# Weight loads placed around the token gathers, and the PSUM banks of the routing stage dealt out anew

## The chip, the cores and the metric

The kernel runs on one core of a Trainium2 chip. The time is device microseconds (us) of one execution, the median of several runs. Engines are named as the profile names them: PE (TensorE, matrix products), DVE (VectorE), ACT (ScalarE), POOL (GpSimd) and SP (SyncE, which issues most DMAs). A bank is one of the eight PSUM banks of 128 x 512 f32.

## The reference

Three layers follow each other: a recurrent attention with gates over 2 x 768 tokens (8 heads of 40), then a mixture of 8 experts in which each expert takes exactly 192 of the 1536 tokens, then a dense mixture of 4 experts.

```python
logits = x @ w_gate                        # x: 1536 x 320, 8 experts
order = np.argsort(-logits.flatten())
for idx in order:                          # best (token, expert) pair first
    tok, e = int(idx) // E, int(idx) % E
    if assigned[tok] >= 0 or counts[e] >= cap:   # cap = 192
        continue
    assigned[tok] = e
    counts[e] += 1
for e in range(E):
    mask = assigned == e
    out[mask] = np.maximum(x[mask] @ w1[e], 0) @ w2[e]      # 320 -> 1024 -> 320
...
p = domain_probs / (domain_probs.sum(-1, keepdims=True) + 1e-09)
for e in range(4):                         # second mixture: all tokens, all experts
    out += p[:, e:e+1] * (np.maximum(x @ w1[e], 0) @ w2[e])
```

## The kernel before, in words

**Three stages.** `attention` writes its rows, padded to 388 columns, to `x_dram` in HBM (L430). `routing` (L617) assigns the tokens, gathers each expert's 192 rows back from `x_dram` and runs the first mixture; its results `X2h` and `X2l` stay in SBUF as two parts of reduced precision. The second mixture (L1262 on) multiplies all tokens by all four experts in three products each.

**The assignment.** There are eight phases, `ph` 0 to 7; a phase fills one expert. `search` (L678) looks for the key value at which one expert reaches 192 tokens, digit by digit, in seven rounds `d`. A round is: twelve small matmuls count tokens above 31 candidates into `pc` (L688); DVE marks which candidates reach 192 in `hit` and `flag` (L709); one matmul with a matrix of ones sums the marks into `pj` (L712), which is the digit; DVE compares the keys with the next candidates around that digit (L719, `cmp`) and then, behind it, moves the base `bt` on to the next digit (L724). In round 5 it forms `kk` (L728) in place of `bt`. `pc` and `pj` are tiles of two banks, `pr` and `pn`. After round 6 the winner is masked out and `offsets` (L810) numbers its tokens. Phase 7 takes what is left (`final`, L819).

**What follows a phase.** `follow` (L1050) runs `dispatch` (L866): it turns the slots into token numbers `tok`, and POOL issues two indirect DMAs (L910, the gathers `xg`, 128 rows of 1552 bytes each). `prep` (L917) transposes the rows on PE (L930) into `xt`. Then `moe1` (L939), a job, has for each of eight blocks `f` of 128 hidden units a product over the last 64 inputs (`thirds`, L953, in two groups of four blocks), two over the first 256 (`main`, L959), a ReLU on ACT (L962), and the second layer (`second`, L972, three blocks behind, and `second3`, L980). The hidden sums `Z` share three banks z0 to z2, and the second group of `thirds` stands behind `main(3)`. The second layer's sums `y0`, `y1` reuse the banks that the job before has left only when DVE has read them for `X2l` (L1003, L1010).

**Weights.** `fetch` (L838), at the end of a search, has SP read the expert's number and issue the load of its first layer's weights (L845, 1280 KB). `fetch2` (L851) issues the second layer's (L857, 1280 KB): right behind for every phase but 0, and in phase 0 between the two gathers, with the number copied by DVE (L854). `split2` (L578) loads the second mixture's weights in pieces `raw` (L592) into six buffers, and splits them on ACT, DVE and POOL. Its first `next` issues the six loads of expert 0; it stands in front of the search of phase 6 (`CR['SP']`, L1185). The loads for expert 1 stand behind everything in `routing` in SP's queue and wait for free buffers only.

**The order.** Each engine runs its instructions in program order. `run` (L1095) and `drain` (L1136) write that order: they keep a reckoned clock of each engine, and put jobs, dispatches and transposes into gaps of the search by assumed costs and due times: `CR['GA']` 3000 ns from a gather's issue to its rows, 1040 ns of POOL for a gather (L915), 5000 ns for the second weights. In phases 0 and 1, while no job exists, PE gaps are filled with dummy matmuls (L1130).

Of the kernel before, what the change touches and what calls it, by code (L numbers as in the profile page):

```python
# [7 lines left out]
F32 = mybir.dt.float32  # L8
F32R = mybir.dt.float32r
BF = mybir.dt.bfloat16  # L10
# [21 lines left out]
BIG = 1e35  # L32
CR = {'D': 0, 'W6': 9, 'SO': 2, 'SC': 3, 'W': 14, 'W0': 5, 'W1': 5, 'W2': 5000, 'W3': (2, 2), 'W4': 4, 'W5': 2, 'X': 4, 'Y': 1, 'L': (6000, 14000), 'GA': 3000, 'WA': 8000, 'VP': 100, 'PV': 190, 'A': (330, 330, 500), 'B': (800, 600, 400), 'SX': 4, 'SP': 6, 'AB': 330}

# [12 lines left out]
def tile_mlstm_moe_moe(ctx: ExitStack, tc: tile.TileContext, gates, gatex, qk, kv, og, wgate, dprob,  # L47
# [26 lines left out]
    cands = [ct([P, NC if d < 6 else 4], BF, name=f"cand{d}") for d in range(1, 7)]  # L74
    onesd = [ct([P, P], BF, name=f"ones{d}") for d in range(6)]
    mask = ct([P, 6], I32, name="mask")
    fold = ct([P, P], name="fold")
    iota16 = ct([P, 16], name="iota16")
# [11 lines left out]
    def routing_consts(pool):  # L90
# [21 lines left out]
        G.memset(crow[0:1, 1:2], float(CAP))  # L112
        G.memset(gone, 0.0)
        for t in cmps + flag + [oa, tk]:
            G.memset(t, 0.0)
        for d, t in enumerate(onesd):
            G.memset(t, 32.0 ** -d)
            G.memset(mask[:, d:d + 1], 31 << (22 - 5 * d) if d < 5 else 3)
        G.memset(erem, float(E1 * (E1 + 1) // 2))
# [27 lines left out]
    last = keys.tile([P, E1], BF, name="last")  # L147
    cmps = [keys.tile([P, NT * NC + P - NC], BF, name=f"cmp{i}") for i in range(2)]
    gone = keys.tile([P, NT], F32, name="gone")
# [467 lines left out]
    def routing():  # L617
        with ExitStack() as st:
# [16 lines left out]

            def pn():
                return ps_r.tile([P, 512], F32, name="pn")

            def side_of(k):
                cmps.reverse()  # L640
                return cmps[0], cmps[0][:, :NT * k].rearrange("p (c k) -> p c k", k=k)

# [7 lines left out]
            def pick(ph):  # L650
# [6 lines left out]
                dgs = pool.tile([P, 6, NT], F32, name="dgs")  # L657
                b1 = pool.tile([P, NT], F32, name="b1")
                kb = top.bitcast(I32)
                out = {"dgs": dgs, "b1": b1}  # L660

                def first():
# [8 lines left out]
                                                      mask[:, :, None].to_broadcast([P, 6, NT]), OP.bitwise_and),  # L671
                              lambda: V.tensor_scalar(dgs, dg, 2.0 ** -27, None, op0=OP.mult),
                              lambda: V.scalar_tensor_tensor(b1, d0, 16.0, dgs[:, 0], op0=OP.add, op1=OP.add)]
                if ph:
# [3 lines left out]
            def search(ph):  # L678
                k = PICK.pop()
                dgs, bt, cmp = k["dgs"], k["b1"], k["cmp"]  # L680
                oh = ohs[ph % 2]
                ready = k.get("ready", clock["V"] + VP)
                for d in range(7):
                    pc = pr()
                    m = NC if d < 6 else 4
                    yield "P", ready - 60, 400 if d < 6 else 280
                    for c in range(NT):
                        T.matmul(pc[:, :E1], cmp[:, m * c:m * c + P], oh[:, c], start=(c == 0), stop=(c == NT - 1))  # L688
                    end = clock["P"] - 80
                    if d == 1:  # L690
                        eo = rt.tile([P, NT, E1], F32, name="eo")
                        V.tensor_mul(eo, oh, bc(erow))
                        on("V", 169)
# [10 lines left out]
                    yield "V", end + PV  # L704
                    pj = pn()
                    if d < 6:
                        fl = flag[d % 2]
                        hit = rt.tile([P, E1], BF, name="hit")
                        V.tensor_scalar(hit[:NC], pc[:NC, :E1], float(CAP), 0.0, op0=OP.is_ge, op1=OP.max,  # L709
                                        accum_out=fl[:NC])  # L710
                        yield "P", on("V", 165) + VP + 30, 110
                        T.matmul(pj[:, 0:1], onesd[d], fl, start=True, stop=True)  # L712
                        yield "V", clock["P"] + PV - 80
                        n = pj[:, 0:1]
                        cand = cands[d]
                        k = cand.shape[1]
                        cmp, v = side_of(k)
                        w = [P, NT, k]
                        V.scalar_tensor_tensor(v, cand[:, None, :].to_broadcast(w), n,  # L719
                                               bt[:, :, None].to_broadcast(w), op0=OP.add, op1=OP.is_le)  # L720
                        ready = on("V", 490 if d < 5 else 190) + 150
                        if d < 5:
                            b2 = rt.tile([P, NT], F32, name="bt")
                            V.scalar_tensor_tensor(b2, bt, n, dgs[:, d + 1], op0=OP.subtract, op1=OP.add)  # L724
                            bt = b2
                        else:
                            kk = rt.tile([P, NT], F32, name="kk")
                            V.tensor_scalar(kk, bt, n, 2.0 ** 31, op0=OP.subtract, op1=OP.mult)  # L728
                        on("V", 150)
# [80 lines left out]
            def offsets(tot, both=True):  # L810
                po = pn()
# [23 lines left out]

            WI, R0 = {}, {}

            def fetch(ph):  # L838
# [7 lines left out]
                XW[ph] = clock["V"] + CR['WA']  # L846
                R0[ph] = r0
                if ph:
                    fetch2(ph)

            def fetch2(ph):  # L851
                if not ph:
                    wi = rt.tile([P, 1], I32, name="wi2", bufs=1)
                    V.tensor_scalar(wi[:1], WI[ph][:1], 0, None, op0=OP.add)  # L854
                    R0[ph] = nc.values_load(wi[0:1, 0:1], engines=[mybir.EngineType.SP], min_val=0,
                                            max_val=(E1 - 1) * P)
                nc.sync.dma_start(W2[ph], m1w2[bass.ds(R0[ph], P), :])  # L857
                XW2[ph] = max(clock["V"] + 1000, XW[ph]) + CR['W2']

# [6 lines left out]
            def dispatch(ph):  # L866
# [41 lines left out]
                for k, (ti, r0, n, s0) in enumerate(pt):  # L908
# [30 lines left out]
            def moe1(ph):  # L939
# [35 lines left out]
                def second3():  # L975
                    for f in range(NF):
                        if f % 4 == 0:
                            yield 1040, H[NF - 1][1]
# [4 lines left out]
                yield from thirds(0)  # L983
# [376 lines left out]
```

## Time and profile before

| | us |
|---|---|
| runs of the kernel | 636.54, 636.74, 651.99 (median 636.74) |
| the profiled execution | 640.5 |
| its span, first to last instruction | 638.4 |
| PE busy | 606.0 (95%) |
| weight loads of PE | 512.7 (80%) |
| DVE busy | 263.4 (41%) |
| ACT busy | 180.5 (28%) |
| POOL busy | 62.9 (10%) |
| chain that ended last: PE 71%, issue 11%, DMA 7%, DVE 6% | |

The busy share of PE is a mean over stages: a slice with the digit 9 in the page's timeline has PE at work nine tenths of the time or more, but at whichever of its two clock levels was granted. The chain of waits is followed back from the last instruction; "DMA xg<-x_dram,tok" has 4% of the span in it.

### The profile page before, as it was taken

What the parts mean: (1) busy time and instruction counts of PE and PEld (TensorE: products, weight loads), DVE (VectorE), ACT (ScalarE), POOL (GpSimd) and SP (SyncE); (2) the same over time, 40 slices, a digit from 0 to 9 for tenths busy, and PEclk for the clock granted to TensorE, in tenths of its full rate; (3) what the DMA queues carried; (4) which work ended last, traced back from release to release, by engine and by line L of the source; (5) the groups of instructions that cost most, each with busy time, mean ns of one, the idle gap of its engine ahead of it and who ended that gap; (6) DMA issues with size and microseconds to landing.
All of it is one profiled execution on the core that took longest, in us unless ns stands there. A gap on an engine that the chain in (4) does not pass through costs nothing.

```text
span 638.4 us, 11154 instructions
## 1 busy us (share of the span) xinstructions
PE 606.0 (95%) x4475; PEld 512.7 (80%) x4478; DVE 263.4 (41%) x952; ACT 180.5 (28%) x472; POOL 62.9 (10%) x120
## 2 busy tenths in 40 slices
PE   7999899799999796999999999999999999999996
PEld 4889764588778685988888888888888888888886
DVE  7767687456666344012322132413224231312231
ACT  7899210122222133323221123311133211111120
POOL 4000001011101113001200001100011000002022
PEclk9999899699999898899999999999999999999999
DMA  7855412435443647201220002300000000001011
GB/s 198 246 138 139 116 38 92 149 142 190 183 174 120 278 177 303 82 1 34 66 84 1 1 0 68 97 17 1 1 1 2 1 1 0 1 1 41 1 42 41
DMA packets 13883, 52.18 MB, mean 82 GB/s; under 512 B 3592, under 2 KB 5544, under 8 KB 11240
## 3 DMA queue, kind: packets, MB, share of 16 engines
q1 hardware_dynamic: 11864, 46.16, 21.6%
q0 software_dynamic: 1600, 5.15, 2.5%
q8 instruction: 35, 0.57, 0.4%
q10 hardware_dynamic: 368, 0.17, 0.1%
q14 instruction: 16, 0.13, 0.1%
HBM read 46.99 MB, written 4.35 MB: 80 GB/s over the span
## 4 chain that ended last, share of the span: by engine, by line
PE 71%; issue 11%; DMA 7%; DVE 6%; ACT 2%; POOL 1%; POOLq 0%; SPq 0%; DVEq 0%; ACTq 0%
PE y L1236 9%; PE y L1238 8%; PE y L1237 8%; PE z L1220 7%; PE z L1222 7%; PE z L1221 6%; PE y L972 4%; DMA xg<-x_dram,tok 4%; PE z L959 4%; PE z L1224 3%; PE px L372 3%; PE z L1229 2%; PE st L336 2%; PE pr L688 2%; DMA raw<-in_m2w_dram 1%
## 5 line engine op out<-in xcount | busy, mean ns | idle before, releaser
L1278 DVE SCALAR_TENSOR_TENSOR h2l<-z,h2h 128x512 fp32r<-128x512 f32 x96 | 66.4, 692 | 238.6 <-ACT h2h L1277 238.6
L1277 ACT ACTIVATE h2h<-z 128x512 fp32r<-128x512 f32 x96 | 57.5, 599 | 262.7 <-PE z L1224 192.2
L1236 PE MATMUL y<-wh,h2h 128*128 128x320 f32 x384 | 120.9, 315 | 0.0
L1238 PE MATMUL y<-wh,h2l 128*128 128x320 f32 x384 | 118.5, 309 | 0.0
L1237 PE MATMUL y<-wl,h2h 128*128 128x320 f32 x384 | 118.5, 309 | 0.0
L1236 PEld LDWEIGHTS y<-wh,h2h 128*128 128x128 f32 x384 | 72.0, 188 | 11.2 <-issue 7.9
L1220 PE MATMUL z<-X2h,wh 128*128 128x512 f32 x192 | 76.9, 401 | 0.8 <-DVE X2l L1010 0.8
L1222 PE MATMUL z<-X2h,wl 128*128 128x512 f32 x192 | 75.9, 395 | 0.0
L1221 PE MATMUL z<-X2l,wh 128*128 128x512 f32 x192 | 75.7, 394 | 0.0
L1237 PEld LDWEIGHTS y<-wl,h2h 128*128 128x128 f32 x384 | 72.1, 188 | 3.2
L1238 PEld LDWEIGHTS y<-wh,h2l 128*128 128x128 f32 x384 | 72.1, 188 | 0.0
L959 PE MATMUL z<-xt,w 128*128 128x192 f32 x256 | 59.7, 358 | 0.0
L972 PE MATMUL y<-h,w 128*128 128x192 f32 x256 | 56.9, 344 | 2.0 <-DVE X2l L1003 2.0
L959 PEld LDWEIGHTS z<-xt,w 128*128 128x128 f32 x256 | 45.3, 205 | 1.8 <-issue 0.7
L972 PEld LDWEIGHTS y<-h,w 128*128 128x128 f32 x256 | 41.8, 193 | 4.0 <-DVE X2l L1003 2.6
L1222 PEld LDWEIGHTS z<-X2h,wl 128*128 128x128 f32 x192 | 36.2, 189 | 9.3
L962 ACT ACTIVATE h<-z 128x192 f32<-128x192 f32 x64 | 21.2, 331 | 79.1 <-PE z L959 74.2
L611 POOL TENSOR_TENSOR wl<-raw,wh 128x512 fp32r<-128x512 f32 x16 | 20.6, 1286 | 232.5 <-ACT wh L601 215.5
L1220 PEld LDWEIGHTS z<-X2h,wh 128*128 128x128 f32 x192 | 36.0, 188 | 6.3 <-DVE X2l L1010 1.1
L1221 PEld LDWEIGHTS z<-X2l,wh 128*128 128x128 f32 x192 | 36.1, 188 | 4.5
L1224 PE MATMUL z<-X2h,wh 128*128 128x512 f32 x96 | 38.0, 396 | 0.0
L688 PEld LDWEIGHTS <-cmp 128*128 128x128 bf16 x588 | 20.4, 98 | 11.6 <-DVE cmp L719 6.1
(260 smaller groups left out, 774.5 us busy)
## 6 DMA issues: line engine op xcount, KB each, us to landing
w<-in_m1w_dram SPq DMA_DIRECT2D x16, 1280.0 KB, 6.4
raw<-in_m2w_dram SPq DMA_DIRECT2D x20, 512.0 KB, 9.4
qk<-in_qk_dram SPq DMA_DIRECT2D x4, 832.0 KB
kv<-in_kv_dram SPq DMA_DIRECT2D x5, 648.0 KB, 5.2
x_dram<-xr SPq DMA_DIRECT2D x12, 194.0 KB, 2.3
qk<-in_qk_dram SPq DMA_DIRECT2D x4, 416.0 KB
sig<-in_og_dram SPq DMA_DIRECT2D x1, 1280.0 KB
raw<-in_m2w_dram SPq DMA_DIRECT2D x4, 256.0 KB, 8.6
```

The costliest lines, as they stand in the source:

```text
L688: T.matmul(pc[:, :E1], cmp[:, m * c:m * c + P], oh[:, c], start=(c == 0), stop=(c == NT - 1))
L959: T.matmul(Z[f], w1[:, k * F + f * P:k * F + (f + 1) * P], xt[:, k], start=False, stop=(k == 1), skip_group_check=True)
L972: T.matmul(Y[0][:, i * CAP:(i + 1) * CAP], w2[:, f * DM + i * P:f * DM + (i + 1) * P], h, start=(f == 0 and i == 0), stop=(f == NF - 1), s ...
L1220: T.matmul(z, hi[:, c], xh[:, k], start=(opens and k == 0), stop=False, skip_group_check=True)
L1221: T.matmul(z, hi[:, c], xl[:, k], start=False, stop=False, skip_group_check=True)
L1222: T.matmul(z, lo[:, c], xh[:, k], start=False, stop=False, skip_group_check=True)
L1224: T.matmul(z, hi[:, c], xh[:, 2], start=False, stop=not opens, skip_group_check=True)
L1236: T.matmul(y[:, :DM], hh[:, ts], hi[:, c], start=(f == 0), stop=False)
L1237: T.matmul(y[:, :DM], hh[:, ts], lo[:, d], start=False, stop=False)
L1238: T.matmul(y[:, :DM], hl[:, ts], hi[:, c], start=False, stop=(f == NF - 1))
L1277: A.activation(hh, z, AF.Relu)
L1278: V.scalar_tensor_tensor(hl, z, 0.0, hh.bitcast(F32), op0=OP.max, op1=OP.subtract)
```

## The change

- The first `next(spl)`, with the six loads of the second mixture's expert 0, stands in front of the search of phase 0.
- `fetch` issues only the first layer's weights. `fetch2` is called in every phase behind both gathers of `dispatch`; the expert's number is copied on POOL, so that SP waits for POOL there.
- The marks of round `d` are kept in rows 32*(d%4) on of one of two `flag` columns, cleared by DVE in rounds 0 and 4; the counts of the round land in those rows, since the window of `cmp` is moved left by `g` columns. One matmul sums all marks so far with two matrices of ones in place of six. The keys' first three digits are kept as prefixes, so that `bt` is a view in rounds 0 to 2. Round 3 forms `bt` ahead of its comparison and round 5 forms `kk` ahead of it; rounds 3 and 4 add the next digit behind it.
- `pj` is columns 16 to 31 of the round's `pc`, and `pn` is gone; the first expert layer has four banks, z0 to z3. All eight blocks of `thirds` stand at the start of a job.
- The planner's assumed costs of a gather (1250 ns of POOL, 2800 ns to the rows) and of the grouped products change.

```diff
         for t in cmps + flag + [oa, tk]:
             G.memset(t, 0.0)
-        for d, t in enumerate(onesd):
-            G.memset(t, 32.0 ** -d)
-            G.memset(mask[:, d:d + 1], 31 << (22 - 5 * d) if d < 5 else 3)
+        G.memset(onesd[1], 0.0)
+        for d in range(6):
+            G.memset(onesd[d // 4][32 * (d % 4):32 * (d % 4) + 32], 32.0 ** -d)
+            G.memset(mask[:, d:d + 1], -(1 << (22 - 5 * d)) if d < 3 else 31 << (22 - 5 * d) if d < 5 else 3)
...
-                              lambda: V.tensor_scalar(dgs, dg, 2.0 ** -27, None, op0=OP.mult),
-                              lambda: V.scalar_tensor_tensor(b1, d0, 16.0, dgs[:, 0], op0=OP.add, op1=OP.add)]
+                              lambda: V.scalar_tensor_tensor(dgs, dg, 2.0 ** -27, off[:, :, None].to_broadcast([P, 6, NT]),
+                                                             op0=OP.mult, op1=OP.add)]
...
-                        T.matmul(pc[:, :E1], cmp[:, m * c:m * c + P], oh[:, c], start=(c == 0), stop=(c == NT - 1))
+                        T.matmul(pc[:, :E1], cmp[:, 96 + m * c - g:96 + m * c - g + P], oh[:, c], start=(c == 0), stop=(c == NT - 1))
                     end = clock["P"] - 80
+                    if d in (0, 4):
+                        V.memset(flag[d // 4], 0.0)
+                        on("V", 60)
...
-                    pj = pn()
+                    pj = pc[:, 16:32]
                     if d < 6:
-                        fl = flag[d % 2]
+                        fl = flag[d // 4]
+                        r = slice(g, g + NC)
...
-                        T.matmul(pj[:, 0:1], onesd[d], fl, start=True, stop=True)
+                        T.matmul(pj[:, 0:1], onesd[d // 4], fl, start=True, stop=True)
...
+                        if d < 3:
+                            bt = dgs[:, d]
+                        if d == 3:
+                            bt = rt.tile([P, NT], F32, name="bt")
+                            V.scalar_tensor_tensor(bt, dgs[:, 2], n, dgs[:, 3], op0=OP.subtract, op1=OP.add)
+                            on("V", 210)
+                        elif d == 5:
+                            kk = rt.tile([P, NT], F32, name="kk")
+                            V.tensor_scalar(kk, bt, n, 2.0 ** 31, op0=OP.subtract, op1=OP.mult)
+                            on("V", 100)
...
-                        if d < 5:
+                        if d in (3, 4):
                             b2 = rt.tile([P, NT], F32, name="bt")
-                            V.scalar_tensor_tensor(b2, bt, n, dgs[:, d + 1], op0=OP.subtract, op1=OP.add)
+                            V.tensor_add(b2, bt, dgs[:, d + 1])
                             bt = b2
...
-                R0[ph] = r0
-                if ph:
-                    fetch2(ph)
+                XW2[ph] = XW[ph] + CR['W2']
 
             def fetch2(ph):
-                if not ph:
-                    wi = rt.tile([P, 1], I32, name="wi2", bufs=1)
-                    V.tensor_scalar(wi[:1], WI[ph][:1], 0, None, op0=OP.add)
-                    R0[ph] = nc.values_load(wi[0:1, 0:1], engines=[mybir.EngineType.SP], min_val=0,
-                                            max_val=(E1 - 1) * P)
-                nc.sync.dma_start(W2[ph], m1w2[bass.ds(R0[ph], P), :])
-                XW2[ph] = max(clock["V"] + 1000, XW[ph]) + CR['W2']
+                wi = rt.tile([P, 1], I32, name="wi2")
+                G.tensor_scalar(wi[:1], WI[ph][:1], 0, None, op0=OP.add)
+                r0 = nc.values_load(wi[0:1, 0:1], engines=[mybir.EngineType.SP], min_val=0, max_val=(E1 - 1) * P)
+                nc.sync.dma_start(W2[ph], m1w2[bass.ds(r0, P), :])
+                XW2[ph] = max(on("G", 100) + 1000, XW[ph]) + CR['W2']
...
-                    if not ph and not k:
-                        fetch2(ph)
-                    XR[ph, ti] = on("G", 1040, clock["V"] + 200) + CR['GA']
+                    XR[ph, ti] = on("G", 1250, clock["V"] + 200) + CR['GA']
+                fetch2(ph)
...
-                def thirds(f0):
-                    yield 1040, r0
-                    for i in range(2):
-                        z = ps_m.tile([P, 512], F32, name=f"z{(f0 // 2 + i) % 3}")
-                        for j in range(2):
-                            Z[f0 + i + 2 * j] = z[:, j * CAP:j * CAP + CAP]
-                    for f in range(f0, f0 + 4):
+                def thirds():
+                    zs = [ps_m.tile([P, 512], F32, name=f"z{i}") for i in range(4)]
+                    for f in range(NF):
+                        if f % 4 == 0:
+                            yield 1040 - f * 48, r0
                         r = f % 2 * 64
                         c = 2 * F + f // 2 * P
-                        T.matmul(Z[f], w1[r:r + 64, c:c + P], xt[r:r + 64, 2], start=(f < f0 + 2), stop=False,
+                        Z[f] = zs[f % 4][:, f // 4 * CAP:f // 4 * CAP + CAP]
+                        T.matmul(Z[f], w1[r:r + 64, c:c + P], xt[r:r + 64, 2], start=(f < 4), stop=False,
                                  skip_group_check=True)
...
-                    if f == 3:
-                        yield from thirds(4)
...
+            next(spl)
             for ph in range(E1):
-                if ph == CR['SP']:
-                    next(spl)
                 run(search(ph) if ph < E1 - 1 else final(ph), ph)
```

## Rows read from the trace of the kernel before

**Rows 1.** Busy time by stretch, second mixture: us, engines' busy us, PEclk, DMA share.

```profile
286.20:605.80 319.60, 319.59 (x1767) 276.27 (x1768) 92.08 (x155) 70.43 (x122) 24.16 (x27) 1.00 0.07 21
```

**Rows 2.** Waits of PE, 91 to 287 us: us in total, times, longest.

```profile
PE t L930 <- DMA xg<-x_dram,tok: 13.5, 7, 4.6
PE y L972 <- DVE X2l L1003: 2.0, 2, 1.4
```

**Rows 3.** Timeline of PE: start, us; in brackets idle before and releaser.

```profile
117.53 0.48 PE L930 MATMUL t<-ident,xg 128*128 128x128 f32 x1 [3.33 <-DMA xg<-x_dram,tok]
...
218.15 0.69 PE L930 MATMUL t<-ident,xg 128*128 128x128 f32 x2 [4.63 <-DMA xg<-x_dram,tok]
...
254.45 0.66 PE L930 MATMUL t<-ident,xg 128*128 128x128 f32 x2 [4.27 <-DMA xg<-x_dram,tok]
```

**Rows 4.** Timeline of POOL: gathers of phases 0, 3, 5 and 7.

```profile
109.51 1.35 POOL L910 DMA_INDIRECT xg<-x_dram,tok  x1 [17.60 <-DVE wi L854]
111.17 0.95 POOL L910 DMA_INDIRECT xg<-x_dram,tok  x1 [0.31 <-DVE hit L709]
...
173.53 0.95 POOL L910 DMA_INDIRECT xg<-x_dram,tok  x1 [0.30 <-issue]
...
209.81 0.94 POOL L910 DMA_INDIRECT xg<-x_dram,tok  x1 [14.49 <-PE z L959]
...
247.38 0.96 POOL L910 DMA_INDIRECT xg<-x_dram,tok  x1 [2.55 <-DVE tok L907]
```

**Rows 5.** Timeline of SP's queue: weight loads around those gathers.

```profile
110.15 0.35 SPq L857 DMA_DIRECT2D w<-in_m1w_dram  x1
...
203.37 3.03 SPq L592 DMA_DIRECT2D raw<-in_m2w_dram  x6
...
243.23 0.33 SPq L857 DMA_DIRECT2D w<-in_m1w_dram  x1
243.68 53.18 SPq L592 DMA_DIRECT2D raw<-in_m2w_dram  x7
```

**Rows 6.** Tile xg, stretches around the gathers of phases 0, 3, 5, 7.

```profile
DMA to landing us min/median/max: 6.8/7.4/8.0
...
DMA to landing us min/median/max: 3.0/3.1/3.1
...
DMA to landing us min/median/max: 8.0/8.2/8.3
...
DMA to landing us min/median/max: 6.8/6.9/6.9
```

**Rows 7.** Line L857, all eight loads of the second weights.

```profile
DMA to landing us min/median/max: 7.0/7.5/8.0
```

**Rows 8.** Busy time in short stretches, last three columns PEclk, DMA share, GB/s.

```profile
111.00:111.25 0.25, 0.25 (x3) 0.13 (x2) 0.02 (x1) 0.00 (x0) 0.08 (x1) 0.50 2.10 328
176.00:176.25 0.25, 0.25 (x3) 0.25 (x2) 0.25 (x1) 0.00 (x0) 0.00 (x0) 1.00 0.14 50
```

**Rows 9.** Timeline of DVE: the number copied for SP in phase 0.

```profile
109.20 0.13 DVE L854 TENSOR_SCALAR wi<-wi 1x1 int32<-1x1 int32 x1
```

**Rows 10.** Busy time in short stretches: where PEclk falls or rises.

```profile
108.50:109.00 0.50, 0.50 (x9) 0.27 (x6) 0.32 (x3) 0.00 (x0) 0.00 (x0) 0.66 0.10 41
...
125.50:126.00 0.50, 0.50 (x4) 0.50 (x3) 0.22 (x1) 0.33 (x1) 0.00 (x0) 0.78 0.41 82
...
224.00:225.00 1.00, 1.00 (x16) 0.84 (x14) 0.17 (x2) 0.33 (x1) 0.00 (x0) 0.65 0.00 0
...
258.00:259.00 1.00, 1.00 (x6) 1.00 (x5) 0.00 (x0) 0.84 (x4) 0.55 (x1) 0.58 0.00 0
```

**Rows 11.** Timeline of PE: job 0's second layer begins; a group of `thirds`.

```profile
126.29 0.90 PE L972 MATMUL y<-h,w 128*128 128x192 f32 x4
...
274.66 0.92 PE L953 MATMUL z<-xt,w 64*128 64x192 f32 x8
```

**Rows 12.** Timeline of DVE in the search of phase 0: `bt` and `kk`.

```profile
98.09 0.23 DVE L724 SCALAR_TENSOR_TENSOR bt<-bt,pn,dgs 128x12 f32<-128x12 f32 x1
...
100.92 0.23 DVE L728 TENSOR_SCALAR kk<-bt,pn 128x12 f32<-128x12 f32 x1
```

More of the change, by code (lines that the diff above doesn't have):

```diff
@@ L32 @@
 BIG = 1e35
-CR = {'D': 0, 'W6': 9, 'SO': 2, 'SC': 3, 'W': 14, 'W0': 5, 'W1': 5, 'W2': 5000, 'W3': (2, 2), 'W4': 4, 'W5': 2, 'X': 4, 'Y': 1, 'L': (6000, 14000), 'GA': 3000, 'WA': 8000, 'VP': 100, 'PV': 190, 'A': (330, 330, 500), 'B': (800, 600, 400), 'SX': 4, 'SP': 6, 'AB': 330}
+CR = {'D': 0, 'W6': 9, 'SO': 2, 'SC': 3, 'W': 14, 'W0': 5, 'W1': 5, 'W2': 5000, 'W3': (2, 2), 'W4': 4, 'W5': 2, 'X': 4, 'Y': 1, 'L': (6000, 14000), 'GA': 2800, 'WA': 8000, 'VP': 100, 'PV': 190, 'A': (330, 330, 500), 'B': (800, 600, 400), 'SX': 4, 'AB': 330}
 def weave(gens):
@@ L74, in tile_mlstm_moe_moe @@
     cands = [ct([P, NC if d < 6 else 4], BF, name=f"cand{d}") for d in range(1, 7)]
-    onesd = [ct([P, P], BF, name=f"ones{d}") for d in range(6)]
+    onesd = [ct([P, P], BF, name=f"ones{d}") for d in range(2)]
     mask = ct([P, 6], I32, name="mask")
+    off = ct([P, 6], name="off")
     fold = ct([P, P], name="fold")
@@ L113, in routing_consts @@
         G.memset(gone, 0.0)
+        G.memset(off, 0.0)
+        G.memset(off[:, :3], 16.0)
         for t in cmps + flag + [oa, tk]:
             G.memset(t, 0.0)
-        for d, t in enumerate(onesd):
-            G.memset(t, 32.0 ** -d)
-            G.memset(mask[:, d:d + 1], 31 << (22 - 5 * d) if d < 5 else 3)
+        G.memset(onesd[1], 0.0)
+        for d in range(6):
+            G.memset(onesd[d // 4][32 * (d % 4):32 * (d % 4) + 32], 32.0 ** -d)
+            G.memset(mask[:, d:d + 1], -(1 << (22 - 5 * d)) if d < 3 else 31 << (22 - 5 * d) if d < 5 else 3)
         G.memset(erem, float(E1 * (E1 + 1) // 2))
@@ L147, in tile_mlstm_moe_moe @@
     last = keys.tile([P, E1], BF, name="last")
-    cmps = [keys.tile([P, NT * NC + P - NC], BF, name=f"cmp{i}") for i in range(2)]
+    cmps = [keys.tile([P, 96 + NT * NC + P - NC], BF, name=f"cmp{i}") for i in range(2)]
     gone = keys.tile([P, NT], F32, name="gone")
@@ L634, in pr @@
                 return ps_r.tile([P, 512], F32, name="pr")
-            def pn():
-                return ps_r.tile([P, 512], F32, name="pn")
             def side_of(k):
                 cmps.reverse()
-                return cmps[0], cmps[0][:, :NT * k].rearrange("p (c k) -> p c k", k=k)
+                return cmps[0], cmps[0][:, 96:96 + NT * k].rearrange("p (c k) -> p c k", k=k)
             def compare(u, cand):
@@ L657, in pick @@
                 dgs = pool.tile([P, 6, NT], F32, name="dgs")
-                b1 = pool.tile([P, NT], F32, name="b1")
                 kb = top.bitcast(I32)
-                out = {"dgs": dgs, "b1": b1}
+                out = {"dgs": dgs}
                 def first():
@@ L679, in search @@
                 k = PICK.pop()
-                dgs, bt, cmp = k["dgs"], k["b1"], k["cmp"]
+                dgs, cmp = k["dgs"], k["cmp"]
                 oh = ohs[ph % 2]
@@ L685, in search @@
                     m = NC if d < 6 else 4
+                    g = 32 * (d % 4) if d < 6 else 0
                     yield "P", ready - 60, 400 if d < 6 else 280
                     for c in range(NT):
-                        T.matmul(pc[:, :E1], cmp[:, m * c:m * c + P], oh[:, c], start=(c == 0), stop=(c == NT - 1))
+                        T.matmul(pc[:, :E1], cmp[:, 96 + m * c - g:96 + m * c - g + P], oh[:, c], start=(c == 0), stop=(c == NT - 1))
                     end = clock["P"] - 80
+                    if d in (0, 4):
+                        V.memset(flag[d // 4], 0.0)
+                        on("V", 60)
                     if d == 1:
@@ L704, in search @@
                     yield "V", end + PV
-                    pj = pn()
+                    pj = pc[:, 16:32]
                     if d < 6:
-                        fl = flag[d % 2]
+                        fl = flag[d // 4]
+                        r = slice(g, g + NC)
                         hit = rt.tile([P, E1], BF, name="hit")
-                        V.tensor_scalar(hit[:NC], pc[:NC, :E1], float(CAP), 0.0, op0=OP.is_ge, op1=OP.max,
-                                        accum_out=fl[:NC])
+                        V.tensor_scalar(hit[r], pc[r, :E1], float(CAP), 0.0, op0=OP.is_ge, op1=OP.max, accum_out=fl[r])
                         yield "P", on("V", 165) + VP + 30, 110
-                        T.matmul(pj[:, 0:1], onesd[d], fl, start=True, stop=True)
+                        T.matmul(pj[:, 0:1], onesd[d // 4], fl, start=True, stop=True)
                         yield "V", clock["P"] + PV - 80
@@ L718, in search @@
                         w = [P, NT, k]
-                        V.scalar_tensor_tensor(v, cand[:, None, :].to_broadcast(w), n,
+                        V.scalar_tensor_tensor(v, cand[:, None, :].to_broadcast(w), 0.0 if d == 3 else n,
                                                bt[:, :, None].to_broadcast(w), op0=OP.add, op1=OP.is_le)
                         ready = on("V", 490 if d < 5 else 190) + 150
-                        if d < 5:
+                        if d in (3, 4):
                             b2 = rt.tile([P, NT], F32, name="bt")
-                            V.scalar_tensor_tensor(b2, bt, n, dgs[:, d + 1], op0=OP.subtract, op1=OP.add)
+                            V.tensor_add(b2, bt, dgs[:, d + 1])
                             bt = b2
[L726 to L729, printed above, removed]
+                            on("V", 80)
                     else:
@@ L810, in offsets @@
             def offsets(tot, both=True):
-                po = pn()
+                po = pr()
                 T.matmul(po[:, 0:2], ones, crow, start=True, stop=False, skip_group_check=True)
@@ L834, in final @@
                 on("V", 200)
-            WI, R0 = {}, {}
+            WI = {}
             def fetch(ph):
@@ L977, in second3 @@
                         if f % 4 == 0:
-                            yield 1040, H[NF - 1][1]
+                            yield 1040 - f * 48, H[NF - 1][1]
                         r = f % 2 * 64
@@ L981, in second3 @@
                                  start=(f < 2), stop=(f >= NF - 2), skip_group_check=True)
-                yield from thirds(0)
+                yield from thirds()
                 for f in range(3):
```

## The prediction

> **What bounds the kernel now.** I read the busy time by stretch first, to find where PE is idle, then PE's waits, then the timelines of the engines that end those waits. From 286 us on PE is busy for 319.59 of 319.60 us at full clock [rows 1]; nothing in the change touches that stretch, so it stays. The stretch in front of it, from the first search at about 92 us, is where the change acts. There one wait stands out: PE's transposes waited 13.5 us, seven times, for gathered rows [rows 2]. Three of those waits make 3.33 + 4.63 + 4.27 = 12.2 us [rows 3]; the other four share 1.3 us. The transposes stand in PE's queue among job and search work, so all of it stops behind them. DVE's chain of search rounds is hidden behind job work from the first job on; it is bare only in phase 0 and in phase 1 up to the first transposes.
>
> Next I looked at why the rows are late. In phase 3 no load runs beside the gathers, and they land 3.0 to 3.1 us after issue. In phases 0, 5 and 7 they take 6.8 to 8.3 us [rows 6], and each of those has weight traffic beside it [rows 4, 5]: in phase 0 the second weights, issued 0.64 us behind the first gather; in phase 5 six `raw` loads queued from 203.4 us in front of the gathers of 209.8; in phase 7 the second weights and the first of the loads for the second mixture's expert 1, issued 4 us ahead of the gather. These stalls cost twice. PE runs at half its clock (1.2 GHz) after them: from 117.53 to about 125.7, from 218.15 to about 224.7, from 254.45 to about 258.8 [rows 3, 10] (a share of 0.78, 0.65, 0.58 in a slice gives the point of the rise). The granted clock also dips at 108.5 us [rows 10], where PE had only small search matmuls: light work costs the clock too.
>
> **The change, part by part.** The sum is made against the profiled execution, 640.5 us with a span of 638.4; it stands 3.8 us (0.6%) above the median of 636.74, to which I apply the same difference.
>
> *Gather stalls.* Moving the six `raw` loads to about 91 us puts them where no other load runs; about 2.8 MB at the 328 GB/s of [rows 8] need some 9 us, so they are in before the first weights are asked for near 104. In SP's queue nothing else stands between; if SP had to wait there for attention's buffers, the first weights still have until the first job, near 117. Phase 5 then has nothing but its first weights, over long before 209.8. In phase 0 the second weights go behind the second gather. In phase 7 SP stops at the number that POOL copies behind the gathers, so the loads for expert 1 stay behind too. Each gather should land in 3.0 to 3.5 us. Phase 0: 109.51 + 3.5 = 113.0, and PE arrives at 117.53 - 3.33 = 114.2: no wait. Phase 5: 209.81 + 3.5 = 213.3 against 213.5: none. Phase 7: 247.38 + 3.5 = 250.9 against 250.2, and the second gather 1.26 us later (0.96 of issue, 0.30 of gap as in [rows 4]): I keep 1.0 us. Of the four small waits I keep all but the 0.35 us that belongs to phase 7, in total 0.9. Gain 13.5 - 1.9 = **11.6**; bounds 10 and 13.5.
>
> *Clock.* The half-rate stretches last 8.2, 6.5 and 4.3 us. If PE alone paced them, half of each would be lost: 4.1, 3.3, 2.2, together 9.6; the lower bound is nothing. In phases 5 and 7 no long idle remains to precede a fall; some of the stretch waited on DVE or on rows, so I take 2.5 and 1.9. In phase 0 light work alone has dropped the clock [rows 10], so I take half, 2.0. Gain **6.4**.
>
> *Fourth bank, `thirds` in one piece.* A second group of eight PE instructions, 0.9 us [rows 11], stands ahead of `second` instead of behind it. PE waited 2.0 us in two places at `second` for DVE's `X2l` [rows 2], the longest 1.4 and so the other 0.6. Both shrink by up to 0.9: gain **1.4**, bounds 0 and 2.0. The products are as many as before; what PE loses on changing between half-height and full products is not counted. A fourth bank costs nothing: all are free long before a job starts, as eight `second` products lie behind the last `main`.
>
> *Search.* Fewer DVE operations behind the comparison are worth nothing: they lie beside the twelve counting matmuls. Two now stand in front of it, `bt` in round 3 and `kk` in round 5, each 0.23 us [rows 12]. Phases 0 and 1 have three to four such places in the open: loss 0 to 0.9, taken **0.5**. In later phases PE has job work to cover them; without that cover it would be another 0.46 per phase. The two clears of `flag` run while DVE waits for counts. The sum in the bank of the counts adds no wait: the next round's counts need the comparison, which is the last reader of the sum.
>
> *Second weights on POOL's word.* The new queue order is gather, gather, copy; SP waits for the copy, and behind it on SP stand only the next phase's first weights (some 10 us later) and, in phase 7, the loads for expert 1, not needed before that expert's turn. POOL's one-element copy is not in the trace; DVE's takes 0.13 [rows 9], POOL's gap between issues 0.30: between these. From DVE's copy to SP's issue it took 0.82 us [rows 5, 9], and bytes moved 0.85 later at the earliest [rows 8]. So the first byte comes 0.95 + 0.13 to 0.30 + 0.82 + 0.85 = 2.75 to 2.9 us after the second gather's issue. A free gather's last bytes pass 2.7 us after its issue (176.2 - 173.53). That is a close pass; I charge **0.5** in total, bounds 0 and the rival below.
> When are the weights there? In phase 0 issue is 111.17 + 0.95 + 0.2 + 0.82 = 113.1, landing 5.6 (no load ahead; estimated as 7.5 less a queue of 2) to 8.0 us later [rows 7], 118.7 to 121.1. Job 0's second layer began at 126.29; with stall, clock loss and 0.9 of extra `thirds` it comes near 126.3 - 3.3 - 2.0 + 0.9 = 121.9. No wait, with under 1 us to spare.
>
> **Sum:** -11.6 - 6.4 - 1.4 + 0.5 + 0.5 = -18.4 us; 636.7 - 18.4 = 618.3, forecast **618**.
>
> **Rivals.**
>
> *A, slower: the second weights run into the second gather.* Place: the pass of 2.75 against 2.7 us above. For it: in phase 0 the load's bytes moved together with the gather's and the gather took 8.0 us. Against it: even the fast end comes behind the gather's bytes. If it decides, the stall of 3.3 us recurs in all eight phases, with about 2 us of clock each: 8 x 5.3 = 42, so 618 + 42 = 660. It decides where the load's first byte comes before about 2.5 us; from 18.4 / 5.3 = 3.5 phases on the kernel is slower than before. Chance 0.06.
>
> *B, the new order eats part.* The reckoned costs change, so every transpose and job is placed anew; PE meets rows or weights a little early several times, and the clock of phase 0 stays low. Eight waits of 0.5 us and 4 us of clock give 618 + 8 = 626. For it: four small waits exist now. Chance 0.15.
>
> *C, the loads are not what delays the gathers.* Suppose gather and load share the queues fairly. A gather is 128 x 1552 bytes, 0.2 MB, 0.6 us at 328 GB/s [rows 8]; at half that rate 1.2. Sharing would explain 0.6 of the 5 us, and the rest would stay: three times 0.6 gained, 636.7 - 1.8 - 1.4 + 0.5 = 634. The Trainium skill says this in DMA: Bandwidth & Descriptors, section Queues, rings and completion order: each engine takes turns between its queues packet by packet. By that rule the trace disagrees: 8.0 beside loads, 3.1 without. In phases 0, 5 and 7 the delay is tied to loads each time [rows 5, 6], so 0.04.
>
> *D, the moves don't do what they say:* the `raw` loads held back into the first weights, or job 0 waiting for its second weights. Some 7 us of the phase-0 and clock terms go: 625. Chance 0.03, within B's range.
>
> **How the numbers follow.** Forecast 0.72, A 0.06, B 0.15, C 0.04, D 0.03. The forecast's own range is 636.7 - 13.5 - 9.6 - 2.0 = 611 or a little less, to 636.7 - 10 - 3 + 1.5 = 625. The range 610 to 630 takes in B and D and leaves out A, C and the ends. This kernel's measurement tells about 2% from no change, so faster means under 624: most of the forecast's case, a little of B: 0.74. Within 2%, up to 649.5: the rest of B, C, D, and A if it decides in a few phases: 0.21. Slower 0.05.
>
> **What would show it.** Right: landing times of all gathers near 3 to 3.5 us; PE's waits at L930 under 3 us in total; full clock through phases 5 and 7; the `raw` loads of expert 0 in SP's queue near 91 us, those of expert 1 behind the last second weights; the second mixture starting near 268 us in place of 286. Wrong: second gathers at 6 us or more (A); PE idle at `second` for DMA in phase 0 (D); gathers late with no load beside them (C); half clock between 112 and 126 again, or new small waits (B).

## The result and the profile after

The changed kernel takes 617.23 us (median of four runs, 616.51 to 619.72) against 638.29 for the kernel before on the same chip: ratio 0.9685, 95% interval 0.9645 to 0.9724. In a later series the ratio was 0.9627 (0.9587 to 0.9667). One of the four runs of the kernel before (651.99 us) is a slow one and is left out of the ratio. The forecast was 618, the range 610 to 630. The span of the profiled execution fell from 638.4 to 615.2 us.

The waits of PE from 91 to 270 us, which answer to [rows 2]; columns are us in total, times, longest:

```profile
PE y L1010 <- ACT ys L1003: 0.9, 2, 0.4
PE z L1222 <- DVE X2l L1013: 0.8, 1, 0.8
...
PE t L936 <- DMA xg<-x_dram,tok: 0.3, 1, 0.3
```

The 13.5 us of waiting for gathered rows are down to 0.3, and the 2.0 us at the second layer for `X2l` are gone. The landing times of all sixteen gathers, which answer to [rows 6]:

```profile
DMA to landing us min/median/max: 3.0/3.4/4.2
```

SP's queue, which answers to [rows 5]: the six loads of expert 0 first, each phase's second weights seven to eleven us behind its first, and the loads of expert 1 behind the last of them:

```profile
91.82 3.01 SPq L596 DMA_DIRECT2D raw<-in_m2w_dram  x6
104.68 0.36 SPq L856 DMA_DIRECT2D w<-in_m1w_dram  x1
114.22 0.35 SPq L864 DMA_DIRECT2D w<-in_m1w_dram  x1
...
131.16 0.34 SPq L864 DMA_DIRECT2D w<-in_m1w_dram  x1
...
239.56 0.34 SPq L864 DMA_DIRECT2D w<-in_m1w_dram  x1
239.99 3.32 SPq L596 DMA_DIRECT2D raw<-in_m2w_dram  x6
```

The close pass of the prediction, in phase 1: POOL issues the second gather and copies the number; a busy-time row at a quarter of a us shows the gather's bytes end and the load's begin (last columns: PEclk, DMA share, GB/s).

```profile
129.21 0.95 POOL L917 DMA_INDIRECT xg<-x_dram,tok  x1 [0.30 <-PE z L964]
130.18 0.21 POOL L862 TENSOR_SCALAR wi<-wi 1x1 int32<-1x1 int32 x1
```

```profile
131.75:132.00 0.25, 0.25 (x3) 0.25 (x2) 0.25 (x1) 0.00 (x0) 0.00 (x0) 1.00 0.11 37
132.00:132.25 0.25, 0.25 (x3) 0.03 (x1) 0.25 (x2) 0.00 (x0) 0.00 (x0) 1.00 2.15 369
```

The load's first bytes come 2.8 us after the gather's issue (132.0 - 129.21), just as the gather's end: the estimate was 2.75 to 2.9 against 2.7.

The clock, which answers to [rows 10]:

```profile
111.50:112.00 0.50, 0.49 (x3) 0.21 (x3) 0.28 (x1) 0.00 (x0) 0.26 (x1) 0.50 0.15 33
114.50:115.00 0.50, 0.50 (x3) 0.15 (x2) 0.20 (x3) 0.00 (x0) 0.00 (x0) 0.75 0.38 115
116.00:117.00 1.00, 0.68 (x16) 0.45 (x15) 0.60 (x2) 0.33 (x1) 0.00 (x0) 1.00 1.01 399
218.00:219.00 1.00, 1.00 (x11) 0.94 (x10) 0.54 (x5) 0.45 (x2) 0.00 (x0) 1.00 0.58 82
```

The half clock of phase 0's light work is still there, between about 111.3 and 114.8; behind it PE keeps 2.4 GHz to the end of the stage. In another execution of the same kernel (e9) it is not: there the granted clock is 1.00 from 104 to 128 us.

Where the time came from is read best from one mark per job: PE's `fold_in` product, the last of a job. Before and after (timeline of PE):

```profile
142.83 0.57 PE L1007 MATMUL y<-ys,fold 128*128 128x192 f32 x2
...
203.79 0.59 PE L1007 MATMUL y<-ys,fold 128*128 128x192 f32 x2
231.76 0.49 PE L1007 MATMUL y<-ys,fold 128*128 128x192 f32 x2
249.37 0.49 PE L1007 MATMUL y<-ys,fold 128*128 128x192 f32 x2
271.21 0.49 PE L1007 MATMUL y<-ys,fold 128*128 128x192 f32 x2
284.81 0.59 PE L1007 MATMUL y<-ys,fold 128*128 128x192 f32 x2 [0.43 <-ACT ys L1000]
```

```profile
137.31 0.57 PE L1010 MATMUL y<-ys,fold 128*128 128x192 f32 x2
...
195.05 0.57 PE L1010 MATMUL y<-ys,fold 128*128 128x192 f32 x2
214.75 0.57 PE L1010 MATMUL y<-ys,fold 128*128 128x192 f32 x2
231.08 0.59 PE L1010 MATMUL y<-ys,fold 128*128 128x192 f32 x2 [0.43 <-ACT ys L1003]
248.78 0.59 PE L1010 MATMUL y<-ys,fold 128*128 128x192 f32 x2
261.66 0.59 PE L1010 MATMUL y<-ys,fold 128*128 128x192 f32 x2 [0.43 <-ACT ys L1003]
```

| stretch | before | after | difference | moves of loads alone (e3) |
|---|---|---|---|---|
| start to first gather | 109.51 | 110.45 | +0.9 | +0.9 |
| first gather to fold of job 0 | 33.3 | 26.9 | -6.5 | -6.0 |
| fold 0 to fold 3 | 61.0 | 57.7 | -3.2 | +0.1 |
| fold 3 to 4 (stall of phase 5) | 28.0 | 19.7 | -8.3 | -7.1 |
| fold 4 to 5 | 17.6 | 16.3 | -1.3 | +0.1 |
| fold 5 to 6 (stall of phase 7) | 21.8 | 17.7 | -4.1 | -5.2 |
| fold 6 to 7 | 13.6 | 12.9 | -0.7 | 0.0 |
| fold 7 to the end | 353.6 | 353.5 | 0.0 | 0.0 |

The three stretches with a long stall give 18.9 us; the others give 5.2, where the forecast had put 0.9. The second mixture starts at 263.1 us; near 268 was forecast.

### The profile page after: what moved, and what is told of

It is laid out like the page before. It is cut to its first block, busy times and chain, and to the rows that moved or that the text cites. A ratio compares the mean times of both kernels' runs of the same rounds, so it can differ in the third digit from the quotient of the medians.

```text
span 615.2 us, 11212 instructions
## 1 busy us (share of the span) xinstructions
PE 598.3 (97%) x4479; PEld 506.7 (82%) x4482; DVE 261.9 (43%) x944; ACT 179.3 (29%) x472; POOL 67.7 (11%) x131
## 4 chain that ended last, share of the span: by engine, by line
PE 59%; issue 3%; DMA 1%; POOL 1%; ACT 1%; DVE 1%; POOLq 0%; ACTq 0%
PE y L1238 9%; PE y L1240 8%; PE y L1239 8%; PE z L1222 7%; PE z L1224 7%; PE z L1223 7%; PE z L1226 3%; PE z L964 2%; PE z L1231 2%; PE y L977 2%; DMA xg<-x_dram,tok 1%; POOL out_dram L1250 1%; PE z L958 1%; PE y L985 1%; PE y L1010 0%
## 5 line engine op out<-in xcount | busy, mean ns | idle before, releaser
L977 PE MATMUL y<-h,w 128*128 128x192 f32 x256 | 55.5, 337 | 0.0
L964 PE MATMUL z<-xt,w 128*128 128x192 f32 x256 | 53.4, 334 | 0.0
L964 PEld LDWEIGHTS z<-xt,w 128*128 128x128 f32 x256 | 42.0, 190 | 0.0
L917 POOL DMA_INDIRECT xg<-x_dram,tok x16 | 17.7, 1106 | 119.0 <-DVE pid L701 33.6
```

The costliest lines, as they stand in the source:

```text
L964: T.matmul(Z[f], w1[:, k * F + f * P:k * F + (f + 1) * P], xt[:, k], start=False, stop=(k == 1), skip_group_check=True)
L977: T.matmul(Y[0][:, i * CAP:(i + 1) * CAP], w2[:, f * DM + i * P:f * DM + (i + 1) * P], h, start=(f == 0 and i == 0), stop=(f == NF - 1), s ...
```

## Experiments

**e1 and e2: each move of loads alone, in the kernel before.**

```diff
-'SP': 6
+'SP': 0
```

> Kernel before with one edit: the six loads of the second mixture's expert 0 in front of the search of phase 0. Theory (loads beside a gather hold its rows back): the stall of phase 5 (4.6 us) and the half clock behind it (2.5 us) go, those of phases 0 and 7 stay: 7 us less, ratio 0.989. Rival 1 (the loads are not what delays gathers): the rows of phase 5 still land after 7 us or more, ratio 0.998 to 1.0. Rival 2 (the new order and the banks bring most of the gain): ratio 0.995 or above.

Measured: ratio 0.9933 (0.9887 to 0.9979), some 4 us. Less than the 7 expected, though the interval reaches it. In its trace, in which the first gather comes late, at 121.0 us, the stall of phase 5 is gone: fold 3 to fold 4 takes 20.8 us in place of 28.0. Those of phases 0 and 7 stay, at 3.2 and 3.5. Rival 1 falls; rival 2's 0.995 lies inside the interval.

```diff
-                if ph:
-                    fetch2(ph)
...
-                    if not ph and not k:
-                        fetch2(ph)
                     XR[ph, ti] = on("G", 1040, clock["V"] + 200) + CR['GA']
+                fetch2(ph)
```

> Kernel before with one edit: the second weights of every phase behind both gathers, on POOL's word. Theory: stalls of phases 0 and 7 (3.3 and 4.3 us) and the half clock behind them (2 and 1.9) go, phase 5 keeps its stall: 10 to 11 us less, ratio 0.983. Rival 1: phases 0 and 7 still wait, ratio 0.998. Rival 2: 0.995 or above. Rival 3 (the second weights run into the second gather): second gathers land after 6 us or more, ratio above 1.0.

Measured: ratio 0.9811 (0.9759 to 0.9863), 12 us. The stalls of phases 0 and 7 shrink to 0.7 and 1.2 us. Phase 5, which should have kept its stall, has little of it left (timeline of PE):

```profile
210.83 0.44 PE L925 MATMUL t<-ident,xg 128*128 128x128 f32 x2 [1.26 <-DMA xg<-x_dram,tok]
...
212.50 0.44 PE L925 MATMUL t<-ident,xg 128*128 128x128 f32 x2 [0.48 <-DMA xg<-x_dram,tok]
```

The six `raw` loads land 10.1 us after their issue here and 14.3 to 14.4 in the kernel before, where phase 5's second weights stand ahead of them in the queue; the gathers land 5.9 us after theirs in place of 8.0 to 8.3. Fold 3 to fold 4 takes 23.1 us here, 20.8 in e1 and 20.9 in e3, which has both moves. So either move alone gives most of that stretch's 7 us, this one 4.9, and the two don't add. Rival 3 falls.

**e3: both moves and nothing else.** Edits of e1 and e2 together.

> Kernel before with both moves of loads and nothing else. Theory: the two gains add, 17 to 18 us, ratio 0.972, leaving about 0.004 for search, banks and assumed costs. Rival 2: half of the whole gain at most, ratio 0.984 or above.

Measured: ratio 0.9798 (0.9724 to 0.9872), 13 us by the runs. By the traces it is 17.1 (638.4 to 621.3), of which the table's last column shows the place: the three long stalls, and nothing else. The interval of the runs reaches rival 2's 0.984, so it is the trace that speaks against it. The rest of the change is worth more than the 0.004 expected: 0.9798 against 0.9685 and 0.9627 for the whole.

**e4: all but the moves.** The changed kernel with `next(spl)` in front of phase 6 and `fetch2` where it was.

> Changed kernel with both loads back where they were before: what is left is the search in row groups, the shared bank, the fourth bank with all third-part products at the start of a job, and the planner's new assumed costs. Theory: 1 to 3 us less than before, ratio 0.996 to 0.998, with the three long stalls at the gathers there again. Rival 2: 10 us or more, ratio 0.984 or below.

Measured: ratio 0.9890 (0.9845 to 0.9935), 7 us, between theory and rival 2. The product 0.9798 x 0.9890 = 0.969 is the whole change. PE's waits (columns as above) keep the rows' stalls and have no wait for `X2l` at the second layer:

```profile
PE t L941 <- DMA xg<-x_dram,tok: 10.2, 5, 3.4
PE y L1015 <- ACT ys L1008: 0.9, 2, 0.4
```

My term for this part was 0.9 us; the next two runs look for the other 6.

**e5: the third-part products as before, in the changed kernel.**

```diff
-                def thirds():
-                    zs = [ps_m.tile([P, 512], F32, name=f"z{i}") for i in range(4)]
+                def thirds(f0):
...
                     yield from main(f)
+                    if f == 3:
+                        yield from thirds(4)
...
```

> Changed kernel with the third-part products as before: two groups of four blocks, the second behind main(3), three banks in turn (z3 is gone), same assumed cost of 1040 ns each. Theory (the part of the gain that the moves of loads leave over is in these products: 0.5 us per job for one change less between half-height and full products, and 2.0 us of waiting for X2l): 5 to 6 us slower than the changed kernel, and the wait of second for X2l is back at 2 us. Rival (planner's new placing and the search bring it): within 1 us of the changed kernel.

Measured: ratio 0.9801 (0.9683 to 0.9920), against 0.9685 and 0.9627 with them in one piece; the interval is wide, but the traces agree: fold 0 to fold 7 takes 130.3 us here and 124.35 in the changed kernel, 5.9 more. PE's waits:

```profile
PE y L978 <- DVE X2l L1009: 4.4, 3, 1.6
PE t L900 <- DVE oa L896: 2.0, 2, 1.7
PE t L936 <- DMA xg<-x_dram,tok: 1.4, 4, 0.5
```

The wait for `X2l` is back, at 4.4 us where 2 were expected. How much of the 5.9 is waiting is told by PE's busy time from fold 0 to fold 7 (busy time by stretch: the stretch, its length, PE's busy time; e5, then the changed kernel):

```profile
135.78:266.08 130.30, 122.72 (x1187) 106.92 (x1186) 66.26 (x355) 37.60 (x109) 20.43 (x24) 1.00 0.46 163
```

```profile
137.31:261.66 124.35, 121.93 (x1192) 106.29 (x1188) 64.61 (x356) 36.91 (x109) 20.77 (x24) 1.00 0.48 170
```

PE idles 7.6 us here and 2.4 in the changed kernel: 5.2 us of the difference are waiting and 0.8 are busy time. The rival falls too: e3 and e5 both have the moves and the old products and differ in the search with its bank and the assumed costs, and they take 129.9 and 130.3 us from fold 0 to fold 7, with ratios of 0.9798 and 0.9801.

The theory's other part, one change of form less, is seen where no search is left. The last job from its first third-part product to the end of `second3` takes 14.44 us before (269.94 to 284.38) and 13.95 after (247.28 to 261.23). Before, the two groups of eight stood apart, one here and one as in [rows 11] (timeline of PE, kernel before); after, all sixteen stand in a row (changed kernel, second fence):

```profile
269.94 0.92 PE L953 MATMUL z<-xt,w 64*128 64x192 f32 x8
270.79 0.59 PE L959 MATMUL z<-xt,w 128*128 128x192 f32 x2
```

```profile
247.28 1.57 PE L958 MATMUL z<-xt,w 64*128 64x192 f32 x16
248.78 0.59 PE L1010 MATMUL y<-ys,fold 128*128 128x192 f32 x2
```

Two groups of eight take 0.85 us each from start to next start, sixteen in a row 1.50, and the full products next to a group lose about 0.1 on each side. That is 0.5 us in this job. The theory takes it for all eight, 4 us, and the trace does not bear that out: in the other seven jobs of the changed kernel other products still fall between the two groups, as in job 0 (timeline of PE):

```profile
117.39 0.92 PE L958 MATMUL z<-xt,w 64*128 64x192 f32 x8
118.25 0.46 PE L689 MATMUL pr<-oh,cmp 128*128 128x8 bf16 x12
118.63 0.92 PE L958 MATMUL z<-xt,w 64*128 64x192 f32 x8
```

**e6: the search alone.** The kernel before with marks in row groups and counts and sum in one bank.

```diff
...
-                    pj = pn()
+                    pj = pc[:, 16:32]
...
```

> Kernel before with the search alone changed: marks in row groups, two matrices of ones, counts and sum in one bank; weight loads, third-part products and assumed costs as before. Theory: bt and kk in front of the comparison cost 0.2 us twice per search and show only in phases 0 and 1: 0 to 0.9 us slower, ratio 1.000 to 1.0015. Rival (fewer DVE operations or the single bank bring part of the gain): 3 us less or more, ratio 0.995 or below.

Measured: ratio 0.9998 (0.9969 to 1.0028). Neither a gain nor a loss that can be told; by the runs the rival falls. The one trace is 4.0 us shorter than that of the kernel before (634.4 against 638.4): the stall of phase 7 is 2.2 us in place of 4.3, and fold 0 to fold 3 takes 58.8 in place of 61.0. The runs do not show that as a gain. The two steps in front of the comparison are in the trace of the changed kernel (DVE) and take what was assumed:

```profile
98.12 0.23 DVE L724 SCALAR_TENSOR_TENSOR bt<-dgs,pr 128x12 f32<-128x12 f32 x1 [0.26 <-PE pr L716]
...
101.49 0.24 DVE L728 TENSOR_SCALAR kk<-bt,pr 128x12 f32<-128x12 f32 x1 [0.26 <-PE pr L716]
```

**e7: the idle time filled, in the kernel before.**

```diff
                     p = ps_m.tile([P, 512], F32, name="t" if ph or k0 else "y0")
+                    if (ph, k0) in FILL:      # {(0, 2): 14, (5, 0): 20, (7, 0): 18}
+                        for _ in range(FILL[ph, k0]):
+                            T.matmul(p.rearrange("p (i t) -> p i t", t=P), tri,
+                                     tri[:, None, :].to_broadcast([P, 4, P]), start=True, stop=True)
```

> Kernel before with dummy matmuls (bf16, 512 columns) in PE's queue in front of the stalled transposes: 14 in phase 0, 20 in phase 5, 18 in phase 7, about as long as the stalls of 3.3, 4.6 and 4.3 us at full clock. The stalls stay, the idle time does not. Theory (the half clock behind a stall follows from the idle time and costs 6.4 us in sum): PEclk stays at 1.0 behind 218 and 252 us and mostly behind 116, 6 us less, ratio 0.990. Rival (the clock term is small, since PE waits for DVE and rows in those stretches anyway): ratio 0.997 or above. If the dummies run longer than the stalls: above 1.0.

Measured: ratio 0.9951 (0.9905 to 0.9997), 3 us. The theory's 0.990 lies just outside that interval and the rival's 0.997 inside, so the runs do not decide between them; the trace says more. In phases 5 and 7 the dummies run ahead of the work that stood in front of the stall, nearly all of the wait for rows is gone, and the clock stays at full (busy time by stretch; PEclk is the third column from the right):

```profile
209.00:213.00 4.00, 4.00 (x21) 2.09 (x20) 0.68 (x4) 0.00 (x0) 1.89 (x2) 1.00 0.99 408
219.00:225.00 6.00, 6.00 (x59) 5.42 (x60) 3.13 (x21) 1.45 (x7) 0.00 (x0) 1.00 0.01 5
246.00:250.00 4.00, 4.00 (x21) 1.77 (x18) 2.11 (x4) 0.43 (x2) 0.76 (x1) 1.00 0.99 395
252.00:258.00 6.00, 6.00 (x41) 5.53 (x40) 0.72 (x1) 2.79 (x10) 1.27 (x1) 1.00 0.59 197
```

Fold 3 to 4 takes 24.64 us in place of 27.97, though PE spends 20 dummies of 0.216 = 4.3 us there in place of a stall of 4.6: some 3.0 us are the clock's. Fold 5 to 6 takes 19.74 in place of 21.84, with 3.9 of dummies and 0.7 of wait for 4.6: 2.1 for the clock. In phase 0 the dummies went into the queue earlier than the transposes, at 109.16; a wait of 1.21 us remained and the clock fell all the same, from 118.8 to 125.6. So phase 0's share was not tested by this run.

**e8: the loads run into the second gather, in the changed kernel.**

```diff
-                G.tensor_scalar(wi[:1], WI[ph][:1], 0, None, op0=OP.add)
+                V.tensor_scalar(wi[:1], WI[ph][:1], 0, None, op0=OP.add)
...
+                    if not k:
+                        fetch2(ph)
                     XR[ph, ti] = on("G", 1250, clock["V"] + 200) + CR['GA']
-                fetch2(ph)
```

> Changed kernel with the second weights asked for between the two gathers of every phase, the number copied on DVE: the loads' first bytes then move with the second gather's. Theory (a load whose bytes move with a gather's holds it back by 4 to 5 us): second gathers land after 6 to 8 us, PE waits 2 to 4 us for rows in most phases with half clock behind some of them, 15 to 40 us slower than the changed kernel. Rival (queues share fairly): second gathers land within 4.5 us, less than 5 us slower.

Measured: ratio 1.0257 (1.0088 to 1.0425), 16 us slower than the kernel before and 36 to 40 slower than the changed one. All gathers are late (tile xg), and PE's waits are:

```profile
DMA to landing us min/median/max: 5.4/6.2/7.7
```

```profile
PE t L937 <- DMA xg<-x_dram,tok: 23.3, 8, 3.5
```

The load is issued 0.1 to 0.8 us behind the first gather's issue here, 1.9 to 2.4 behind the second's in the changed kernel. Those two us are worth more than the whole change.

**e9 and e10: the halves of the grouped products in one piece.** e10 is the changed kernel with one planner's piece for all of `thirds` and one for all of `second3`; e9 is the changed kernel beside it.

```diff
-                        if f % 4 == 0:
-                            yield 1040 - f * 48, r0
+                        if f == 0:
+                            yield 1550, r0
...
```

> The changed kernel again, beside the next one on the same chip, to compare the two: ratio 0.968 to 0.972 against the kernel before.

> Changed kernel with all eight blocks of the third-part products, and all eight of second3, given to the planner as one piece each, so that no search matmul falls between their halves. Theory (each change between half-height or half-width and full products costs PE 0.2 us): two changes less in each of the six phases with a search beside the job, 0.4 us each, 2 to 3 us faster than the changed kernel, ratio 0.964 to 0.966. Rival: the longer pieces hold up the search's chain by as much: no difference, or up to 2 us slower.

Measured: e9 0.9627 (0.9587 to 0.9667), below the 0.968 to 0.972 expected; e10 0.9710 (0.9673 to 0.9746). The longer pieces make it slower, by 5 us. Fold 0 to 1 does take 17.6 us in place of 19.2, but the transposes now come close together and wait for ACT to free their bank, and for rows:

```profile
PE t L936 <- ACT xt L937: 2.7, 5, 0.6
PE t L936 <- DMA xg<-x_dram,tok: 1.6, 4, 0.9
```

These waits were 0 and 0.8 us in e9. From fold 0 to fold 7 PE is busy 1.5 us less than in e9 (120.5 against 122.0), which would be about 0.12 us for each of twelve changes of form saved, and idle 3.1 us more (5.6 against 2.5). That leaves 1.6 us lost there by the traces; where the rest of the 5 us goes stays open. No version here beats the changed kernel.

## Why the prediction was right, and where not

- **Gather stalls (11.6 us): right.** From 13.5 us of waiting to 0.3. I had kept 1.9; so 13.2. The cause is shown in both directions: with the loads kept behind them the gathers land in 3.0 to 4.2 us, and e8 puts the delay into all eight phases.
- **Clock (6.4 us): right for phases 5 and 7, low for phase 0.** Taken 2.5 and 1.9; e7 gives 3.0 and 2.1. For phase 0 I took half, 2.0, because light work had dropped the clock without a stall. The stretch from first gather to fold 0 gave 6.5, of which the stall was 3.33; some 3 are left for the clock, a little more for what the search cost. That share is read from a difference of traces, not isolated. The row of the light work was misread, too: at 108.5 us PE had not only small search products, since dummy matmuls of 512 columns (L1130) start at 105.91 and 108.57, with waits of 0.17 and 0.33 us between them. In e9 the clock does not dip there, so what brings the dip stays open.
- **The two moves in sum: right.** -11.6 - 6.4 + 0.5 = -17.5 forecast; 17.1 between the traces of before and e3, 13 between the runs (interval 8 to 18). That they overlap in phase 5 (e2) I had not seen: I put that stall down to the `raw` loads, where the second weights ahead of them in the queue had their part: with those behind the gathers 4.9 us of that stretch go, though the `raw` loads stay.
- **Fourth bank and `thirds` in one piece (1.4 us): mis-sized, by the waiting above all.** I counted the 2.0 us of waiting for `X2l` in the trace before, and wrote that "what PE loses on changing between half-height and full products is not counted". e5 puts the term at 5.9 us: with the old order PE waits 4.4 us for `X2l` and idles 5.2 more in all, while its busy time differs by 0.8. Measured from e3 instead it is 5.6 us, 3.6 of them waiting. The change of form that I left out is 0.5 us in the one job where the two groups come to stand in a row. Why the wait is 4.4 us in e5 and 2.1 in e3 is not shown.
- **Search (0.5 us lost): right within what can be told**, e6 0.9998. The four small pieces that DVE lost behind the comparison brought nothing that the runs show.
- **Second weights (0.5 us for the close pass): nearly nothing.** The pass held in all phases, with POOL's copy at 0.21 to 0.23 us. Rival A was priced at 42 us above the forecast for eight phases; forced in e8, it costs 36 to 40. Of B's new small waits for rows there is one of 0.3 us, and D's wait at `second` for weights is not there.
- **Rival C** falls by e8, which delays every gather by loads alone. Its 0.6 us is the price of equal shares of the bytes, and taking turns by packets is another thing. In the changed kernel from 127 to 136 us the two gathers are 128 packets with 0.40 MB, the load some 139 with 1.30 MB; turns would leave a gather about a quarter of some 400 GB/s, which makes an estimate of 1.5 us more. e8's median is 2.8 us above the changed kernel's (6.2 against 3.4), so turns alone fall short by this estimate but are not refuted, and my "the trace disagrees" said too much. In the same section the Trainium skill (DMA: Bandwidth & Descriptors, Queues, rings and completion order) also says that an engine's increment of a semaphore lands only after every earlier write of that engine, across its queues. Rows that come in only when the load is through would agree with that: in e8's phase 1 the load lands at 141.3 us and the gathers at 141.5 and 141.8. No run here separates it from a slow share of the queue.
- **The sum** of 18.4 us stands against 20.1 by the ratio of the first series and 23.8 by the second. By the traces the moves were right (17.1) and e5's 5.9 come on top, together 23.0 of the 23.2 us between the spans. By the runs the two errors cancel: the moves gave some 13 where 17.5 were put, the rest some 7 where 0.9 was. So that the time came out so near 618 is in part luck. A trace is one execution, and most executions of the kernel before in one series lie between 632 and 642 us, so sums from two traces carry a few us of that. The far end of the forecast's own range took 3 us as the least for the clock, though its lower bound had been put at nothing; with nothing that end is 628 in place of 625, still inside 630.

## What to carry to other kernels

Look at what is on the queues while a small transfer that an engine waits for is under way: here 1.3 MB of weights and more, needed only later, made a gather land 2 to 5 us later, and half the PE clock followed most of those waits. A load whose bytes start where the gather's end cost next to no wait here; the two us between the two issues are the issue of the gather (0.95), a one-element copy behind it on the same engine (0.21), and 0.77 from the copy's end to SP's issue. And when a group of products is moved, look in the new trace at whether it stands where it was meant to, and at the waits it fills: here the two groups still stood apart in seven of eight jobs, and most of the 5.9 us that the move gave were waiting.

## What had not been expected

- e2: a load that was thought harmless, since it stood far ahead of the gather, did its harm through the queue, by holding back six others, which landed 14.3 us after their issue in place of 10.1.
- Clock behind short waits: in e7 a wait of 1.21 us, one of 0.35 and small matmuls around them were followed by half clock from 118.8 to 125.6 us, while in the changed kernel a wait of 0.32 us at the same place was not.
- The attention stage in front varies between executions of one kernel: the first gather of the changed kernel was issued at 110.45 us in one trace and at 114.16 in another (e9). The +0.9 us at the head of the table is within that, and no effect of the change can be read from it.
